# One folded weight by seven half-block products per pair of rows, in an mLSTM cell followed by a multiplicative feed-forward kernel

## The chip, the core and the metric

The kernel runs on one core of a Trainium2 chip. The metric is the device time of one execution in microseconds (us). Engines are named as the profile names them: PE is TensorE's matrix multiply and PEld its weight loads, DVE is VectorE, ACT is ScalarE, POOL is GpSimd, SP is the engine that issues most DMAs. PSUM is the memory that PE writes its results to.

## The reference, cut to what matters

The first half is a recurrent cell over 768 time steps for 4 batches of 8 heads of width 40. The second half is a feed-forward block with weights alone between its products:

```
C = f_stab * C + i_stab * outer(v_t, k_t);  n = f_stab * n + i_stab * k_t
y_t = sigmoid(o_t) * (C q_t) / max(|n . q_t|, 1)
...
x = y as (3072 tokens, 320)
a = x @ w1            # w1, w2: 320 x 1024
b = x @ w2
h = a * b @ w3        # (a * b) @ w3, w3: 1024 x 1024
return h @ w_out      # w_out: 1024 x 320
```

There is nothing between `w3` and `w_out`, so the kernel computes the product `w3 @ w_out` once (1024 x 320, "the folded weight", `w3o`) and applies it to `a * b`.

## The kernel before, in words

**Tiling.** The cell is computed chunkwise: 24 units of 128 time steps of one batch (6 chunks of time by 4 batches). The feed-forward block has 6 groups of 512 tokens. `up` and `up_rest` compute a and b for two 128-row slices of the 1024 and 256 tokens: two products of 128 rows per slice in `up`, and the last 64 of the 320 rows in `up_rest`, which packs four 64x64 products into the array at once. The result `ab` is multiplied into the output by `w3o` in `ffn_out`. Groups 3 to 5 are computed in another way (`up_by_seven`, `out_by_seven`): a 2x2 split of the matrices, whose product is made of seven half-size products and 15 sums instead of eight products (Strassen's method in Winograd's form). Every PE product in float32 shows in the trace as two weight loads and two matmul records; a transpose shows as one of each.

**Folding.** `w_out` lies in `wo`, eight tiles of 128 rows. `w3` arrives in 16 half tiles of 64 rows (the weights are 64-bit floats in memory: `fetch` issues the DMAs, four for a half of `w3`, into one of four `raw` buffers; `scale` works on both words on ACT; `to_f32` joins them on DVE, L199 and L200). `convert` then turns a half of `w3` on DVE (L248) into `w3T[ko]`; there are two `w3T` buffers. One step after both halves of a tile are turned, `fold` makes its 128 rows of the folded weight: eight products 128x128 by 128x320 that accumulate in one PSUM tile (`w3_mm`), and one ACT copy into `w3o` (L264). Eight tiles give 64 products, 128 records.

**Stages and order.** A loop over 32 steps s overlaps everything. In step s, PE does in order: transposes of y of an earlier unit (`x_trans`, px), the folds, output products, the `up` blocks, their `up_rest`, and then `quarter_work`, which has the cell's many small products for units s and s-1. The lists below give how many blocks, output products and conversions each step has:

```python
n_up = [0] * 2 + [1] * 4 + [2] * 10 + [0] * 16
n_down = [0] * 16 + [2] * 5 + [1] * 4 + [0] * 7
n_cvt = [0, 0, 2, 0, 1, 2, 3, 3, 3] + [2] * 6
```

PE runs in the order in which the program is written (`in_order` adds an ordering dependency between each two products), and `keep_order` does the same for the other engines at the end. `issue_after` only places instructions behind a given one in that order; it adds no wait across engines. So each engine is a queue that runs in program order, and a wait at its head holds what stands behind it. The conversions of step s come at its end, and DVE does them while PE is in step s+1. A step's weights are fetched four conversions ahead (`fetched < converted + 4`).

**PSUM.** Before step 24 the `mps` tiles (pa, pb, px, wp, po) share four banks; a tile takes the bank that is free the longest and waits until its last reader is done with it. The reader of pa is ACT (a_sb, L638), of pb it is DVE (ab, L639).

**POOL** has, in each step of this part: a state update (L335) that waits for DVE's update of the state, the weighted v for the next unit (vw, L330), a small copy of y (L476), two causal masks on pw for the next unit (L308), and the state update at the head of the next step.

In the profile of before, `quarter_work`'s products begin on PE at 48.2 us in step 4, 55.8 in step 5, 93.1 in step 8, 105.4 in step 9, 125.8 in step 10, 141.1 in step 11, 203.0 in step 15 and 218.2 in step 16.

Of the kernel before, what the change touches and what calls it, by code (L numbers as in the profile page):

```python
# [8 lines left out]
FP = mybir.dt.float32  # L9
# [7 lines left out]
def kernel(  # L17
# [59 lines left out]
    def mps(shape, name):  # L77
        pool = banks.pop(0)
        banks.append(pool)
        return pool.tile(shape, FP, name=name, tag="m")  # L80
# [10 lines left out]
    def mm(out, lhsT, rhs, start=True, stop=True):  # L91
        in_order(nc.tensor.matmul(out, lhsT=lhsT, rhs=rhs, start=start, stop=stop))  # L92
# [135 lines left out]


    w3T_t = {}  # L230
    turned_w3, ready_w3 = [], []

    def scale_next(early=False):
        scaled.append(pend.pop(0))
# [2 lines left out]
    def convert():  # L237
        if not scaled:
            scale_next()
        dst, raw, ko, half = scaled.pop(0)  # L240
        if dst is not None:
            to_f32(dst, raw)
            return
        w3 = wst.tile([128, CW], FP, name="w3", tag="w3")
        to_f32(w3, raw)
        if half == 0:
            w3T_t[ko] = wst.tile([128, FO, 128], FP, name="w3T", tag="w3T")
        nc.vector.transpose(out=w3T_t[ko].rearrange("c k (m r) -> c m k r", r=32)[:, 2 * half:2 * half + 2],  # L248
                            in_=w3.rearrange("r (m c k) -> r m k c", m=2, k=FO))
        if half:  # L250
            turned_w3.append(ko)

    def fold():
        while ready_w3:
            w3_mm(ready_w3.pop(0))
        ready_w3.extend(turned_w3)
        turned_w3.clear()

    def w3_mm(ko):
        w3T = w3T_t.pop(ko)  # L260
        wp = mps([128, DM], "wp")
        for ki in range(FO):
            mm(wp, w3T[:, ki, :], wo[:, ki, :], start=(ki == 0), stop=(ki == FO - 1))
        nc.scalar.mul(out=w3o[:, ko, :], in_=wp, mul=UP ** -2)  # L264


    qT_t, kT_t, vw_t, before_t, y_t, x_t = {}, {}, {}, {}, {}, {}
# [65 lines left out]
    def decayed(new, old, n, x):  # L333
        c, b = divmod(n, B)
        nc.gpsimd.tensor_tensor(out=new, in0=old, op=OP.mult, in1=decay[:, b * NP:(b + 1) * NP, 2 * c + x:2 * c + x + 1]  # L335
                                .to_broadcast([P, NP, D1]))
# [281 lines left out]
    def up(gr, fs, cs):  # L618


        if gr not in ab_t:
            ab_t[gr] = [ffn.tile([128, FO, 2 * P], FP, name="ab", tag="ab", bufs=6) for _ in range(2)]
        x, n = x_t[gr], cs.stop - cs.start
        pa, pb = mps([128, len(fs), n], "pa"), mps([128, len(fs), n], "pb")
        for p, wt in ((pa, w1), (pb, w2)):
            for i, f in enumerate(fs):
                for cc in range(KF):
                    mm(p[:, i, :], wt[:, cc, f * 128:(f + 1) * 128], x[:, cc, cs], start=(i == cc == 0), stop=False)
        return pa, pb, x, gr, fs, cs

    def up_rest(pa, pb, x, gr, fs, cs):
        for i, f in enumerate(fs):
            for j, e in quarters:
                mm((pa, pb)[j][halves[e], i, :], wr[halves[j], f * 128 + e * L:f * 128 + (e + 1) * L],
                   x[halves[j], KF, cs], start=False, stop=(i == len(fs) - 1))
        j, t0 = divmod(cs.start, 2 * P)
        a_sb = ffn.tile([128, len(fs), cs.stop - cs.start], FP, name="a_sb", tag="a_sb")
        nc.scalar.mul(out=a_sb, in_=pa, mul=UP ** -2)  # L638
        nc.vector.tensor_tensor(out=ab_t[gr][j][:, fs[0]:fs[-1] + 1, t0:t0 + a_sb.shape[-1]], in0=pb, in1=a_sb, op=OP.mult)  # L639
# [90 lines left out]

        return single, shared, left, product

    def ffn_out(blocks, pos=None):

        pos = pos or [mps([P, DM], "po") for _ in blocks]
        for (gr, j), po in zip(blocks, pos):
            for f in range(FO):
                mm(po, ab_t[gr][j // 2][:, f, j % 2 * P:(j % 2 + 1) * P], w3o[:, f, :], start=(f == 0), stop=(f == FO - 1))
        for (gr, j), po in zip(blocks, pos):
            o_sb = ffn.tile([P, DM], FP, name="o_sb", tag="o_sb", bufs=2)  # L740
            nc.scalar.copy(out=o_sb, in_=po)  # L741
            t0 = j * S + gr * P
            nc.scalar.dma_start(out=out[t0:t0 + P, :], in_=o_sb)


    KH, NH = FO // 2, DM // 2

    def out_weight_sums():

        T_o.extend(m[:, i * KH * NH:(i + 1) * KH * NH].rearrange("p (f n) -> p f n", n=NH)  # L750
                   for m, i in ((v_all, 0), (gates, 0), (gates, 1), (q_all, 0)))
        (B11, B12), (B21, B22) = ([w3o[:, k * KH:(k + 1) * KH, i * NH:(i + 1) * NH] for i in range(2)] for k in range(2))
        T1, T2, T3, T4 = T_o
        for dst, p, q in ((T1, B12, B11), (T2, B22, T1), (T3, B22, B12), (T4, B21, T2)):
            yield nc.gpsimd.tensor_tensor(out=dst, in0=p, in1=q, op=OP.subtract)

    T_o, S_o = [], {}
    wsums = out_weight_sums()

    def quarters_of_ab(gr, j):  # L760
        return [[ab_t[gr][j][:, k * KH:(k + 1) * KH, t * P:(t + 1) * P] for k in range(2)] for t in range(2)]
# [49 lines left out]
    n_out = [0] * 27 + [1, 0, 1, 0, 3]  # L811
    w12 = [("w12", i, part) for part in range(2) for i in range(2 * KF + 1)]
    todo = w12[5:] + [("wo", i, 0) for i in range(FO)] + [("w3", ko, part) for ko in range(FO) for part in range(2)]
    n_cvt = [0, 0, 2, 0, 1, 2, 3, 3, 3] + [2] * 6
    n_fetch = [5, 5, 10]
    pinned, ahead = 32, 9
    behind = ExitStack()
# [2 lines left out]
    for s in range(len(n_up)):  # L820
# [21 lines left out]
        if s < NU:  # L842
            if s >= B:
                decayed(state[s % B][1], state[s % B][0], s, 0)
        if s == 2 or N_DVE < s < NY + 2:
            twice(s - 2)
        if NY <= s - 2 < NU:
            get_back(s - 2)
        while s >= N_DVE and turned < min(s - 2, NY):
            x_trans(turned)  # L850
            turned += 1
        fold()
        if s >= len(n_up) - 2:
            ab_sums(*summed.pop(0))
        def pairs():
# [13 lines left out]
            seven[1]()  # L869
        if seven and s <= NU:  # L870
            ffn_out([downs.pop(0) for _ in range(n_down[s])], [cell[1][:, i, 0:DM] for i in range(2)])
        else:
            for _ in range(n_down[s]):
                ffn_out([downs.pop(0)])
# [2 lines left out]
        if seven and s > NU:  # L877
            seven[0]()
        now = [ups.pop(0) for _ in range(n_up[s])]
        open_ups = [up(*x) for x in now] if s != 2 else []  # L880
        if s == 3:
            turn(3)
        def rest():
            for x in open_ups:
                up_rest(*x)
            if seven:
                seven[2]()
            if s == 3:
                scale_next()
                scale_next()  # L890

        def between():
            twice(1)
            weighted(2)
            rows_of_u(3)
            for _ in range(3):
                scale_next()
            for n in range(2):
                x_trans(n)
                if n == 0:  # L900
                    warm(1, small=38)
            for _ in range(3):
                convert()
            turn(2)
            block = up(*now[0])
            weighted(3)
            weights(3)
            masks(3)
            out_gate(2)
            convert()  # L910
            up_rest(*block)

        gated = None
        if s <= NU:
            gated = quarter_work(s, rest, between if s == 2 else None, convert if s == 3 else None)
        else:
            rest()
        with tc.issue_after(gated.ins) if gated else nullcontext():
            if seven:
                seven[3]()  # L920
            for _ in range({NU: 1, NU + 1: 3}.get(s, 0)):
                next(wsums)
            if s == NU + 1:
                ab_sums(*summed.pop(0))
            if NY <= s - 2 < NU:
                x_turn(s - 2)
            for n in () if s == 1 else (s + 2,) if s < B else (s + 2, s + 3) if s == B else (s + 3,):
                if n < N_U:
                    rows_of_u(n)
            if N_DVE <= s + 1 < NU:  # L930
                gated = turn(s + 1)
            if s - 2 in range(4 * GT - 1, NU, GT):
                token_sums((s - 2) // GT)
            if s < len(n_up) - 2 and n_out[s + 1] and s > NU + 2:
                ab_sums(*summed.pop(0))
# [28 lines left out]
        if s == B:  # L964
            for i, r in enumerate(third):
                nc.sync.dma_start(out=U_d[i * GC:(i + 1) * GC].rearrange("c r t -> r c t"), in_=U3[r])
        with tc.issue_after(gated.ins) if N_DVE <= s + 1 < NU else nullcontext():
            for _ in range(n_cvt[s] if s < len(n_cvt) else 0):
                convert()
                converted += 1  # L970
# [9 lines left out]
            for ins in keep_order(front):  # L980
                behind.enter_context(tc.issue_after(ins))
    behind.close()
    assert not ups and not sevens and not downs and not outs and not summed and not todo and not pend and not turned_w3 and not ready_w3, (len(ups), len(downs), len(todo), len(pend))
# [1 line left out]
_INS = ['q', 'k', 'v', 'i_gate', 'f_gate', 'o_gate', 'moe_w1', 'moe_w2', 'moe_w3', 'moe_w_out']  # L985
_OUTS = [((3072, 320), 'float32')]
# [25 lines left out]
```

## Time and profile before

| what | value |
|---|---|
| time, median of 3 runs | 426.7 us (424.85, 426.7, 532.37) |
| profiled execution, its own time | 427.89 us |
| its span, first to last instruction | 425.8 us |
| granted TensorE clock over the span | 0.996 |
| PE busy | 414.1 us, 97% of the span, 5353 records |
| DVE / POOL / ACT busy | 74% / 36% / 35% |
| the fold, wp<-wo,w3T | 128 records, 35.9 us busy |
| up_rest, pa and pb<-xT,wr | 768 records, 73.4 us busy |
| w3o<-wp on ACT (L264) | 8 copies, 438 ns each |
| w3T<-w on DVE (L248) | 16 turns, 1111 ns each |
| instruction DMAs (queue q8) | 42 packets, 0.69 MB |
| mean DMA rate | 120 GB/s; 183 GB/s from 30 to 108 us |

In an answer of the trace, a row of the timeline has the start in us, the length in us, the engine, the line, the operation, out<-in, the shape and the number of records that were merged. A bracket at its end gives how long the engine was idle just before, and what ended that. Matmul records overlap, so a row is longer than the time that it adds: the distance between the starts of two rows is the time PE gave to the first. "issue" is time in which an engine waited for nothing that the profile shows. Line numbers are those of the kernel before.

### The profile page before, as it was taken

How to read it: one execution, taken by the hardware profiler on the slowest of the kernel's cores; microseconds unless marked ns; L12 is line 12 of the kernel's file. 1: busy time of each engine (PE TensorE's matmuls, PEld its weight loads, DVE VectorE, ACT ScalarE, POOL GpSimd, SP SyncE). 2: the span in 40 equal slices, each digit the busy share in tenths (PEclk: the TensorE clock that was granted, in tenths of full speed). 3: DMA queues.
4: the chain of work that ended last, by engine and by line, in shares of the span. 5: the costliest groups of instructions: out<-in, count | busy, mean ns of one | idle time of the engine just before them, and what ended most of it. 6: DMA issues, size and time to landing. Idle time of an engine off the chain costs nothing.

```text
span 425.8 us, 13079 instructions
## 1 busy us (share of the span) xinstructions
PE 414.1 (97%) x5353; PEld 335.3 (79%) x5353; DVE 313.5 (74%) x635; ACT 150.1 (35%) x404; POOL 154.3 (36%) x211
## 2 busy tenths in 40 slices
PE   7989989999999999999999999999999999999996
PEld 4768878888688788787777778788778879888896
DVE  6676986888949779778736966596868699575971
ACT  4766865567723623630433313032311110210000
POOL 4421342233303303303307751546453587542100
PEclk9989999999999999999999999999999999999999
DMA  8999998598977776985425675756421120000001
GB/s 186 204 173 245 214 144 140 134 193 180 215 183 154 166 182 135 181 164 105 89 80 130 153 141 121 142 133 117 87 44 36 35 39 2 31 2 31 2 32 62
DMA packets 135211, 51.15 MB, mean 120 GB/s; under 512 B 109360, under 2 KB 126960, under 8 KB 135152
## 3 DMA queue, kind: packets, MB, share of 16 engines
q1 hardware_dynamic: 131552, 46.29, 53.9%
q10 hardware_dynamic: 3600, 4.03, 2.7%
q8 instruction: 42, 0.69, 0.7%
q14 instruction: 17, 0.14, 0.1%
HBM read 44.50 MB, written 5.80 MB: 118 GB/s over the span
## 4 chain that ended last, share of the span: by engine, by line
PE 53%; issue 20%; DVE 7%; POOL 7%; SPq 7%; DMA 5%; ACT 1%; POOLq 0%; DVEq 0%
PE cell L92 17%; PE pa L92 12%; PE o L92 8%; PE pb L92 8%; PE p L92 3%; POOL pw L308 3%; SPq L184 3%; DVE w3T L666 2%; PE pt L95 1%; POOL vw L330 1%; SPq L148 1%; DMA raw<-in_moe_w_dram 1%; PE fill L92 1%; POOL raw L659 1%; POOL state L335 1%
## 5 line engine op out<-in xcount | busy, mean ns | idle before, releaser
L335 POOL TENSOR_TENSOR state<-state,decay 128x164 f32<-128x164 f32 x40 | 20.0, 500 | 154.8 <-DVE state L404 129.0
L92 PE MATMUL pa<-xT,w 128*128 128x256 f32 x240 | 60.4, 382 | 0.0
L92 PEld LDWEIGHTS pa<-xT,w 128*128 128x128 f32 x240 | 44.4, 190 | 6.8 <-DVE h L430 0.4
L303 ACT ACTIVATE pw<-pw,aT 128x64 f32<-128x64 f32 x184 | 46.4, 339 | 3.2 <-ACT o_sb L741 1.9
L92 PE MATMUL pb<-xT,w 128*128 128x256 f32 x192 | 45.4, 379 | 0.0
L729 POOL TENSOR_TENSOR ab<-ab,a_sb 128x512 f32<-128x512 f32 x22 | 29.4, 1356 | 32.2 <-DVE ab L684 32.2
L92 PEld LDWEIGHTS pb<-xT,w 128*128 128x128 f32 x192 | 36.4, 190 | 5.0
L711 POOL TENSOR_TENSOR wo<-wo 128x512 f32<-128x512 f32 x22 | 27.4, 1268 | 29.8 <-DVE wo L686 29.8
L92 PE MATMUL pa<-xT,wr 64*64 64x256 f32 x384 | 37.0, 386 | 0.5 <-DVE wr L200 0.5
L92 PE MATMUL wp<-wo,w3T 128*128 128x320 f32 x128 | 35.9, 433 | 1.1 <-DVE ab L639 0.6
L308 POOL TENSOR_SCALAR_AFFINE_SELECT pw<-pw 64x512 f32<-64x512 f32 x48 | 35.8, 746 | 3.0 <-ACT pw L303 1.2
L92 PE MATMUL pb<-xT,wr 64*64 64x256 f32 x384 | 36.4, 380 | 0.0
L92 PE MATMUL cell<-w3o,ab 128*128 128x320 f32 x128 | 35.4, 432 | 0.0
L638 ACT ACTIVATE a_sb<-pa 128x512 f32<-128x512 f32 x24 | 14.3, 598 | 59.0 <-PE pb L92 59.0
L639 DVE TENSOR_TENSOR ab<-pb,a_sb 128x512 f32<-128x512 f32 x24 | 16.4, 688 | 23.2 <-ACT a_sb L638 22.8
L92 PEld LDWEIGHTS wp<-wo,w3T 128*128 128x128 f32 x128 | 23.8, 190 | 10.5 <-DVE ab L639 0.8
L92 PEld LDWEIGHTS cell<-w3o,ab 128*128 128x128 f32 x128 | 24.3, 190 | 9.5
L92 PEld LDWEIGHTS pa<-xT,wr 64*64 64x64 f32 x384 | 18.9, 132 | 15.4 <-issue 8.8
L686 DVE SCALAR_TENSOR_TENSOR a_sb<-pa,wo 128x512 f32<-128x512 f32 x12 | 8.3, 689 | 29.8 <-PE pa L92 29.8
L430 DVE TENSOR_TENSOR h<-cell,h 64x164 f32<-64x164 f32 x88 | 28.6, 326 | 1.6
L92 PE MATMUL po<-w3o,ab 128*128 128x320 f32 x96 | 26.4, 433 | 0.0
L92 PEld LDWEIGHTS po<-w3o,ab 128*128 128x128 f32 x96 | 18.1, 190 | 7.3
(180 smaller groups left out, 846.4 us busy)
## 6 DMA issues: line engine op xcount, KB each, us to landing
raw<-in_moe_w_dram SPq DMA_DIRECT2D x64, 128.0 KB, 3.4
kbuf<-in_k_dram SPq DMA_DIRECT2D x24, 160.0 KB, 4.5
v_all<-in_v_dram SPq DMA_DIRECT2D x24, 160.0 KB, 4.9
o_in<-in_o_gate_dram SPq DMA_DIRECT2D x24, 160.0 KB, 4.8
pw<-U_d SPq DMA_DIRECT2D x28, 128.0 KB, 3.5
raw<-in_moe_w_dram SPq DMA_DIRECT2D x5, 512.0 KB, 6.7
raw<-in_moe_w_out_dram SPq DMA_DIRECT2D x8, 320.0 KB, 4.1
gates<-in_k_dram SPq DMA_DIRECT2D x28, 80.0 KB, 2.5
```

Of the source, the lines that this page charges most:

```text
L92: in_order(nc.tensor.matmul(out, lhsT=lhsT, rhs=rhs, start=start, stop=stop))
L184: nc.sync.dma_start(out=dst, in_=src)
L303: nc.scalar.activation(out=pw[:, h, :], in_=src[:, h, :], func=AF.Exp, bias=aT[:, c, b * H + h:b * H + h + 1])
L308: nc.gpsimd.affine_select(out=pw[r], in_=pw[r], compare_op=OP.is_ge, fill=0.0, base=0, pattern=[[0, H], [1, L]], channel_multiplier=-1)
L335: nc.gpsimd.tensor_tensor(out=new, in0=old, op=OP.mult, in1=decay[:, b * NP:(b + 1) * NP, 2 * c + x:2 * c + x + 1] .to_broadcast([P, NP, D1]))
L430: nc.vector.tensor_tensor(out=part, in0=ph[x][halves[e]], in1=part, op=OP.add)
L638: nc.scalar.mul(out=a_sb, in_=pa, mul=UP ** -2)
L639: nc.vector.tensor_tensor(out=ab_t[gr][j][:, fs[0]:fs[-1] + 1, t0:t0 + a_sb.shape[-1]], in0=pb, in1=a_sb, op=OP.mult)
L666: nc.vector.tensor_tensor(out=dst, in0=p, in1=q, op=OP.subtract)
L686: nc.vector.scalar_tensor_tensor(out=out, in0=p, scalar=UP ** -2, in1=q, op0=OP.mult, op1=OP.add)
L711: aside_by.tensor_tensor(out=kept[j][:, 1:4:2], in0=kept[j][:, 1:3], in1=kept[j][:, 3:4].to_broadcast([128, 2, TH]), op=OP.add)
L729: aside_by.tensor_tensor(out=t[:, f:FO:FH, :], in0=t[:, f:FO:FH, :], in1=a, op=OP.mult)
```

## The change

**The fold.** The rows of `w3o` are made in four pairs i of tiles (2i, 2i+1) by the seven-product method. The 2x2 split is: two tiles, two halves of the 1024 (four products deep each), and two halves of the 320 columns. Each of the seven products is four PE products 128x128 by 128x160. The parts are:

- four sums of `wo` on POOL, once (`fold_weight_sums`, each 128x640: two in step 8, two in step 9). One of them overwrites a quarter of `wo`, one lies in the memory of `w3o`'s last pair until that pair is made; for that pair the fourth sum is made again (`fold_last_sum`, step 15).
- four sums of `w3T` on POOL per pair (`fold_sums`, each 128x512, steps 9, 11, 13, 15). One overwrites a part of `w3T`; the others lie in the `ab` memory of group 2 before that is used, and for the last pair in two `raw` buffers.
- `fold_first(i)`: two of the seven products, behind `quarter_work` of steps 9, 11, 13 and 14, and one ACT copy.
- `fold_second(i)`: the other five, 20 PE products, behind the first `up` block and its `up_rest` of steps 10, 12, 14, and behind the first part of the output products of step 16; two ACT copies; and five sums, on POOL for the first three pairs and on DVE for the last.

**Moved with it.** In steps 10, 12 and 14 the first block's `up_rest` follows its `up` at once instead of standing behind the second block's `up`. `x_trans` of units 7, 9 and 11 moves from the head of a step to behind `quarter_work` of the step before. In step 16 the output products over the last two of eight tiles follow `quarter_work`. The `w3` buffer before the turn is one instead of two, and the output's staging tile lies in the memory of the sums of `wo`.

**One conversion** moves from step 8 to step 5, and with it the fetches of steps 5 to 8, which follow the number of conversions.

**The last rows** of the first blocks (steps 2, 3 and 4) are computed in two parts of 128 columns instead of one of 256.

```diff
-    def fold():
-        while ready_w3:
-            w3_mm(ready_w3.pop(0))
...
-    def w3_mm(ko):
-        w3T = w3T_t.pop(ko)
-        wp = mps([128, DM], "wp")
-        for ki in range(FO):
-            mm(wp, w3T[:, ki, :], wo[:, ki, :], start=(ki == 0), stop=(ki == FO - 1))
-        nc.scalar.mul(out=w3o[:, ko, :], in_=wp, mul=UP ** -2)
+    def fold_weight_sums():
...
+        for dst, p, q in ((T1, B12, B11), (T2, B22, T1), (T4, B21, T2), (B12, B22, B12)):
+            yield nc.gpsimd.tensor_tensor(out=dst, in0=p, in1=q, op=OP.subtract)
+
+    def fold_sums(i):
...
+        (A11, A12), (A21, A22) = rows_of_w3(i)
...
+        for dst, p, q, op in ((S1, A21, A22, OP.add), (S2, S1, A11, OP.subtract), (A21, A11, A21, OP.subtract),
+                              (S4, A12, S2, OP.subtract)):
+            nc.gpsimd.tensor_tensor(out=dst, in0=p, in1=q, op=op)
+
+    def fold_first(i):
+        A11, A12 = (w3T_t[2 * i][:, k * KH:(k + 1) * KH] for k in range(2))
+        (B11, _), (B21, _) = halves_of(wo)
+        wp = fold_products(((A11, B11), (A12, B21)))
+        return lambda: nc.scalar.mul(out=fold_of(i)[:, 0:3:2], in_=wp, mul=UP ** -2)
+
+    def fold_second(i):
...
+        wp, wq = mps([128, 3, NH], "wp"), mps([128, 2, NH], "wq")
+        for p, x, a, b, first, last in ((wq, 1, A22, T4, True, False), (wp, 0, S1, T1, True, False), (wp, 1, S2, T2, False, False),
+                                        (wp, 2, S3, T3, False, True), (wq, 0, S4, B22, False, True)):
+            for k in range(KH):
+                mm(p[:, x], a[:, k, :], b[:, k, :], start=(first and k == 0), stop=(last and k == KH - 1))
...
+        nc.scalar.mul(out=M1, in_=wp, mul=UP ** -2)
+        nc.scalar.mul(out=M2, in_=wq, mul=UP ** -2)
+
+        def adds(by=nc.gpsimd):
+            for out, p, q in ((C[:, 1], M1[:, 1], C[:, 0]), (C[:, 0], C[:, 0], C[:, 2]), (C[:, 2], M1[:, 2], C[:, 1]),
+                              (C[:, 1:4:2], C[:, 1:3], M1[:, 0:1].to_broadcast([128, 2, NH])), (C[:, 1:3], M2, C[:, 1:3])):
+                by.tensor_tensor(out=out, in0=p, in1=q, op=OP.add)
...
-    def up_rest(pa, pb, x, gr, fs, cs):
+    def up_rest(pa, pb, x, gr, fs, cs, parts=1):
+        n = (cs.stop - cs.start) // parts
         for i, f in enumerate(fs):
-            for j, e in quarters:
...
+            for t in range(parts):
+                for j, e in quarters:
+                    mm((pa, pb)[j][halves[e], i, t * n:(t + 1) * n], wr[halves[j], f * 128 + e * L:f * 128 + (e + 1) * L],
...
-    n_cvt = [0, 0, 2, 0, 1, 2, 3, 3, 3] + [2] * 6
+    n_cvt = [0, 0, 2, 0, 1, 3, 3, 3, 2] + [2] * 6
...
+        elif s == 16:
+            finish = ffn_out([downs.pop(0) for _ in range(n_down[s])], split=FO - 2)
+            fold_second(FO // 2 - 1)(nc.vector)
...
+        if s in (10, 12, 14):
+            up_rest(*up(*now.pop(0)))
+            adds.append(fold_second((s - 10) // 2))
...
+                up_rest(*x, parts=2 if s in (3, 4) else 1)
...
+        if s == 16:
+            finish()
+        if s in (9, 11, 13):
+            x_trans(turned)
+            turned += 1
+        if s in (9, 11, 13, 14):
+            first_copy = fold_first((s - 8) // 2)
         with tc.issue_after(gated.ins) if gated else nullcontext():
...
+            if s in (8, 9):
+                next(fsums), next(fsums)
+            for x in adds:
+                x()
+            if s in (9, 11, 13, 15):
+                fold_sums((s - 9) // 2)
```

## The prediction

> **What bounds the kernel now.** I read the engine totals first, then PE's waits, then PE's timeline step by step. Totals, and the stretch in which the fold lies (start:end us, length, busy per engine with records, clock, DMA share, GB/s):
>
> ```profile
> PE 414.1 (97%) x5353; PEld 335.3 (79%) x5353; DVE 313.5 (74%) x635; ACT 150.1 (35%) x404; POOL 154.3 (36%) x211
> ...
> 108.00:205.00 97.00, 96.12 (x1281) 77.14 (x1282) 74.47 (x142) 39.14 (x102) 20.69 (x36) 1.00 0.76 159
> ```
>
> PE idles 0.9 us of these 97, at full clock; POOL has 76 us free. So time here is the sum of PE's records, and an edit pays if it takes records from PE without making it wait. One step without a stall:
>
> ```profile
> 127.66 0.55 PE L95 MATMUL px<-ident,y 128*128 128x128 f32 x3
> 128.04 4.47 PE L92 MATMUL wp<-wo,w3T 128*128 128x320 f32 x16
> 132.35 1.89 PE L92 MATMUL pa<-xT,w 128*128 128x256 f32 x8
> 134.08 1.89 PE L92 MATMUL pb<-xT,w 128*128 128x256 f32 x8
> ```
>
> By starts, px gives PE 0.38 us of work, a tile's fold 4.31 (16 records, 269 ns each), a block's up 3.46. The breaks in PE's stream that this change touches:
>
> ```profile
> 107.65 1.24 DVE L639 TENSOR_TENSOR ab<-pb,a_sb 128x512 f32<-128x512 f32 x2
> ...
> 108.35 1.07 PE L92 MATMUL wp<-wo,w3T 128*128 128x320 f32 x3 [0.58 <-DVE ab L639]
> ...
> 59.05 0.23 PEld L92 LDWEIGHTS cell<-vw,kbuf 64*40 64x40 f32 x12 [1.60 <-issue]
> ...
> 96.51 0.27 PE L95 MATMUL pt<-ident,q_all 128*128 128x128 f32 x1 [0.30 <-issue]
> ...
> 144.57 3.93 PE L92 MATMUL wp<-wo,w3T 128*128 128x320 f32 x14 [0.54 <-issue]
> ```
>
> The first is a PSUM bank: wp waits for DVE's ab, which stands behind step 8's third conversion (its turn of w3T ends at 107.72). From px at 107.22 to wp at 108.35 is 1.13, 0.75 more than usual. The others wait for no engine: they start at 57.37, 95.94 and 143.61, and exceed normal spacing by 1.7, 0.5 and 0.75. In the recorded stream of PE (loads and products) they stand before records 1985, 3265 and 4545, which are 193 + 256 x 7, x 12, x 17. Queue q8 brings 42 packets, 0.69 MB, so 16 KB each. These are instruction refills.
>
> [...] 160-column records follow each other faster than a 190 ns load.
>
> ```profile
> 381.37 2.34 PE L92 MATMUL o<-gates,kbuf 128*128 128x160 f32 x16
> 383.55 1.25 PE L92 MATMUL o<-w3o,ab 128*128 128x160 f32 x8
> ```
>
> That is 2.18/16 = 136 ns. [...]
>
> ```profile
> 364.67 0.59 PE L92 MATMUL pa<-w3T,w 128*128 128x256 f32 x2
> 365.10 0.59 PE L92 MATMUL pb<-xT,raw 128*128 128x256 f32 x2
> 365.63 1.09 PE L92 MATMUL pa<-xT,wr 64*64 64x256 f32 x16
> ...
> 367.51 0.70 PE L92 MATMUL p<-xT,w 128*128 128x256 f32 x2
> 368.05 0.38 PE L92 MATMUL p<-w3T,raw 128*128 128x256 f32 x1
> ```
>
> A pair takes 0.43; before wr it takes 0.53, after it 0.54, and the 32 wr records take 1.88 against 1.71 to 1.73 in their own mode: together 0.36 for a round trip. [...] vw takes 0.73 mostly, but 1.18 at 46.69. [...]
>
> **The change part by part.**
>
> *Fold products.* Removed: 128 records x 269 = 34.5. Added: 4 pairs x 28 products x 2 = 224 records x 136 = 30.5. PE gains 4.0.
>
> *Mode changes.* In steps 10, 12 and 14 the first block's wr stands between products of the full array. Three round trips x 0.36 = +1.1. Elsewhere the new parts join changes that exist.
>
> *x_trans moved* from the heads of steps 10, 12, 14: the same records. The copy on ACT now runs under fold_first (16 x 136 = 2.2 us), which covers its 0.47; without that up would wait some 0.6. Nothing.
>
> *Conversion moved.* In step 5 DVE's third conversion of wo (0.52 + 0.62) and ACT's two passes (2 x 0.49) meet an idle DVE: 2.93 before ab at 69.43. Nothing; without that idle, 1.1. In step 7 two of three are now w3 (2.3 against 1.15), so ab is 1.1 late; its bank is asked for 2 us later, covered. In step 8 DVE loses 2.3 us, so the 0.75 at 107.5 goes: -0.75. The next reader there is fold_first itself, for the same ab, which is then 1 us early. Its fetch, four DMAs, moves from step 8 to before step 7's loads: past pw, kbuf, q_all, v_all and o_in on SP (1.8 us of issue, about 2.6 us of transfer, 0.5 MB at 200 GB/s). SP stood idle from 71.05 to 77.99, and kbuf, issued at 84.17 and landing in a median 5.0, is read by PE at 95.29: 6 us spare. Nothing. On POOL no DMA is moved.
>
> *Sums on POOL.* Per pair 4 x 1.27 (row L711, 128x512), once 4 of 128x640 at 1.5 to 2.0 (four rows of L755), adds of 3 x 0.47 + 2 x 0.73. All 24+ us fit into POOL's free time; what counts is when. Behind the sums on POOL stand vw and the masks of the next unit, read 6 us or more later. Behind px, POOL's state update ends 3.2 us later (94.90 to 98.08 in step 8). In step 9 two weight sums (4.0) and four sums (5.1) follow: S1 at 8.5, S4 at 12.3, some 0.4 later [...]. PE: px 0.38, fold_first 2.2, up 3.55, wr 1.0, so fold_second starts at 7.2, its first product needs T4 alone; it would take S1 at 8.3 and S4 at 11.6. S4 is 0.7 to 1.1 late: +1.0 (bounds 0 and 3.7, the latter with POOL at vw's 1.6 times). For steps 12 and 14 the weight sums are absent, S4 comes at 8.7, and nothing is late.
>
> *Waits on DVE.* Its turn of w3T in step 9 overwrites what the sums read, so waits for S4: about 4 us. Behind it stand a conversion and the first block's ab. In the built order the second block's pb takes the bank that ACT frees, not this ab's; ab is needed by px of step 11, 3 us later. Nothing; in other cover up to 1.4.
>
> *ACT* gets 4 more copies and wider ones, 2.3 us over seven steps at 35% busy. Nothing.
>
> *Step 16.* PE leaves the last two tiles open until DVE's five adds: M1 copied 0.7 after its product (1.1 before fold_second ends), then 3 x 0.33 + 2 x 0.49 and gaps: done about as quarter_work (1.9) ends. +0.2, bounds 0 and 1.
>
> *Last rows in two parts.* 24 products become 48 of half the length. [...] 64-column products already keep pace with their loads. +0.1, bounds 0 and 0.3.
>
> *Refills.* The trace's refill starts 2 to 3.4 us after PE is 64 records ahead of a block, 6.5 at worst (56.6), takes 1.1, and is used 1.4 later: about 5 us, 8.8 at worst. So a block of short records breaks the stream. The work of the three broken ones (64 records and the block) is 7.1, 4.1 and 4.1 us; the next whole one had 5.0. Parts and fold shift the numbering by 96 and 192: in the built program the short ones are in steps 5 (7.2), 6 (5.4), 9 (4.75), 13 (4.5) and 14 (4.85). The one in step 5 meets the same loaded DMA: 1.4; the rest 0.4 + 0.7 + 0.6 + 0.2. Sum 3.3 against 3.0: +0.3, bounds -3.0 and +5.
>
> Sum: -4.0 + 1.1 - 0.75 + 1.0 + 0.2 + 0.1 + 0.3 = -2.0. The profiled execution took 427.9 (span 425.8 and 2.1 around it) and becomes 425.9; the median of 426.7, lower by 1.2, becomes **424.7**.
>
> **Rivals.** (1) The gain is eaten at the fold: [...] S4 is 3.7 late in step 10, not 1.0: 424.7 + 2.7 = 427.4. For it: vw at 1.18; against: 22 sums on L711 averaged 1268. (2) Slower, by refills: five short blocks stand in the loaded half. If a refill takes 6.5 us, the five breaks are 0, 1.1, 1.75, 2.0 and 1.65; with step 5's at its worst 1.6 they make 8.1, 4.8 over my 3.3: 429.5. It decides above 5.5 us; against it are the typical 5 us after 90 us. (3) The numbering falls well and no refill or sum is late: -4.0 + 1.1 - 0.75 + 0.3 - 3.0 = -6.3: 420.4. That the products are not shortened is excluded by the 136 ns.
>
> **Chances.** Forecast 424.7 (422.5 to 426.3): 0.60; gain eaten, about 427.4: 0.19; refills, 428 to 432: 0.15; better, to 420.4: 0.06. The range 421.5 to 429.5 leaves out half of the last two and little else. 2% is 8.5 us, about what a measurement of this kernel can tell from no change: faster needs below 418.2, slower above 435.2. No case reaches the first; the second takes refills near the worst and a stall together, 0.06.
>
> **What would show it.** wp and wq with 224 records at 136 ns; no wp wait for ab near 107; rows "issue" on PE near 57 and 105 to 175, and their sum; PE waiting for POOL's sums in step 10 alone; PE busy about 2.5 us less. I am wrong if 160-column records run slower, if POOL's sums hold PE in steps 12 or 14, or if DVE, held by S4, holds PSUM banks.

## The result, and the profile after

The changed kernel takes 430.26 us, median of 20 runs, against 426.8 us for the kernel before: a ratio of 1.0076, 95% interval 1.0051 to 1.0102, so 2.2 to 4.4 us more. One run of each kernel, at 532.37 and 603.92 us, fell in a slow state and is left out of the ratio. The prediction had 424.7, with a range to 429.5. The profiled execution of the changed kernel took 433.0 us (span 431.3), 2.7 above its median. Where those 2.7 lie is seen below: in the start-up.

Engine totals of the changed kernel: busy time, share of the span, number of records.

```profile
PE 417.5 (97%) x5497; PEld 347.2 (81%) x5497; DVE 328.6 (76%) x640; ACT 152.1 (35%) x408; POOL 199.4 (46%) x247
```

The same stretch as in the prediction, 108 to 205 us, in the view of stretches (start:end us, length, busy per engine with records, in the order PE, PEld, DVE, ACT, POOL, then clock, DMA share, GB/s):

```profile
108.00:205.00 97.00, 92.70 (x1329) 80.97 (x1322) 83.39 (x140) 41.14 (x106) 55.09 (x65) 0.98 0.71 158
```

PE was to be 2.5 us less busy, and shows 3.4 more. It idles 4.3 us of these 97, where it idled 0.9. DVE has 8.9 more to do in them (83.39 against 74.47) and POOL 34.

These two moments are not at the same work, so I cut both executions at three starts that mean the same in both: the second px, the last px ahead of the fold, and the first of the 32 output products that follow the fold. Before, the start-up and the stretch of the fold:

```profile
0.00:28.41 28.41, 23.92 (x407) 15.98 (x407) 20.61 (x53) 17.02 (x51) 11.98 (x41) 0.94 0.94 182
...
94.90:231.03 136.13, 134.72 (x1835) 106.73 (x1827) 99.50 (x194) 56.58 (x152) 35.89 (x57) 1.00 0.70 150
```

The same two after:

```profile
0.00:31.65 31.65, 28.01 (x408) 19.69 (x408) 20.79 (x53) 17.04 (x51) 12.73 (x42) 0.84 0.94 186
...
98.06:236.44 138.38, 134.09 (x1932) 114.20 (x1924) 113.37 (x198) 57.92 (x154) 80.62 (x93) 0.99 0.68 146
```

The start-up took 31.65 against 28.41: 3.2 us of the 5.5 between the spans. In it PE ran at a clock of 0.84, against 0.94 before. In the profiled executions of the experiments, most of which have the start-up of one of the two kernels unchanged, the same px comes at 25.7 to 29.6. So this belongs to the one execution and not to the change. What the change costs stands in the stretch of the fold, 138.38 against 136.13. DVE is 13.9 us busier in it.

PE's timeline of the changed kernel, fold products only (start, length, engine, line, operation, tile and operands, count, and in brackets the idle time ahead with what ended it):

```profile
112.29 4.12 PE L92 MATMUL wp<-wo,w3T 128*128 128x160 f32 x16 [1.83 <-DVE ab L707]
...
145.74 2.44 PE L92 MATMUL wp<-wo,w3T 128*128 128x160 f32 x16 [1.16 <-DVE ab L707]
...
153.78 2.34 PE L92 MATMUL wp<-fold_m,ab 128*128 128x160 f32 x16
155.96 1.25 PE L92 MATMUL wp<-wo,w3T 128*128 128x160 f32 x8
...
177.10 2.44 PE L92 MATMUL wp<-wo,w3T 128*128 128x160 f32 x16 [1.16 <-DVE ab L707]
```

Two lines in the middle show that the products take what was forecast: 155.96 - 153.78 = 2.18 for 16 records, 136 ns each. The other three are fold_first of steps 9, 11 and 13. Each waits for ab, with which DVE reads a block's pb; that it waits for the PSUM bank of pb is tested in experiment 1. By starts, from px to wp, the three take 2.37, 1.71 and 1.70 where 0.38 is normal: 2.0, 1.3 and 1.3 lost. Of these, only a wait of 0.75 had stood in the kernel before, and that one was to go.

The first is also longer than the other two, 4.12 against 2.44. PE's clock between 112 and 116 (third number from the right):

```profile
112.00:116.00 4.00, 3.71 (x16) 3.71 (x17) 3.73 (x12) 1.25 (x5) 0.19 (x1) 0.60 0.76 207
```

The breaks that I take for refills of PE's instructions cost less than forecast in this execution. That they are refills is an inference from counts: queue q8, which the profile lists as "instruction", brings 42 packets in the execution before and 43 in this one, and PE has 10706 and 10994 records of loads and products in them, 41.8 and 42.9 times 256. The breaks of 1.7 near 57, of 0.5 near 96 and of 0.7 near 143 are gone, and there is one new one, at the end of step 6, where one packet of q8 starts between 71 and 73; on PE's load side:

```profile
74.11 0.19 PEld L92 LDWEIGHTS cell<-vw,kbuf 64*40 64x40 f32 x9 [1.54 <-issue]
```

The account of the profiled executions, after less before, in us. "Read" is from starts of PE's groups of records:

| term of the prediction | predicted | read |
|---|---|---|
| fold products, mode changes, step 16 (-4.0 + 1.1 + 0.2) | -2.7 | -2.5 |
| wait of wp for ab | -0.75 | +3.9 (2.0 + 1.3 + 1.3 - 0.75) |
| POOL's sums late in step 10 | +1.0 | +0.3, and 1.7 of half clock ahead of it |
| refills | +0.3 | -1.25 (1.64 new; 1.74, 0.46 and 0.69 gone) |
| last rows in two parts | +0.1 (an estimate) | +0.03 (925 ns against 914, three times) |
| start-up | 0 | +3.2, this execution |
| behind the fold | 0 | +0.1 |
| sum | -2.0 | +5.5 |

The first "read" is what remains of the stretch's +2.25 when 6.6 of waits and half clock in it after, and 1.9 of waits before, are taken off; so the column must add up, and that it does proves nothing. Without the start-up the sum is +2.3, at the low end of the measured 2.2 to 4.4. So the question for the experiments is why ab is late, three times.

**Step 9.** DVE in the changed kernel, from the unit's o_in to ab:

```profile
102.56 1.58 DVE L508 SCALAR_TENSOR_TENSOR o_in<-o_in,den 128x320 f32<-128x320 f32 x1
104.17 1.72 DVE L510 TENSOR_TENSOR y<-h,o_in 128x320 f32<-128x320 f32 x1
...
106.91 1.10 DVE L200 CUSTOM_DVE_ANT_0 w<-raw,w 128x1024 uint16<-128x1024 uint16 x1
...
111.59 1.25 DVE L707 TENSOR_TENSOR ab<-pb,a_sb 128x512 f32<-128x512 f32 x2
```

The same two operations in the kernel before:

```profile
98.35 0.76 DVE L443 SCALAR_TENSOR_TENSOR o_in<-o_in,den 128x320 f32<-128x320 f32 x1
99.15 0.49 DVE L445 TENSOR_TENSOR y<-h,o_in 128x320 f32<-128x320 f32 x1
```

And POOL beside them in the changed kernel:

```profile
102.23 1.56 POOL L266 TENSOR_TENSOR fold_m<-wo 128x640 f32<-128x640 f32 x1
103.87 1.67 POOL L266 TENSOR_TENSOR fold_m<-wo,fold_m 128x640 f32<-128x640 f32 x1
```

o_in and y take 2.05 longer, and each ends 0.35 after one of POOL's two subtractions. Not all of DVE's work is stretched: the transposition kT takes 1.13 beside a sum of POOL (at 119.83; POOL from 119.52, 1.56) where it took 1.10 before. What sets the two kinds apart is not shown. From o_in to ab DVE needs 9.0 us with two conversions; before it needed 9.3 with three, and one conversion is 2.3.

**Steps 11 and 13.** DVE in the changed kernel, from the ab of step 10 to that of step 11:

```profile
132.09 0.69 DVE L707 TENSOR_TENSOR ab<-pb,a_sb 128x512 f32<-128x512 f32 x1 [2.04 <-ACT a_sb L706]
132.69 0.49 DVE L488 TENSOR_TENSOR h<-cell,gT 128x328 f32<-128x328 f32 x1
...
145.04 1.25 DVE L707 TENSOR_TENSOR ab<-pb,a_sb 128x512 f32<-128x512 f32 x2
```

The same work in the kernel before, with the last row of its conversions:

```profile
127.31 0.49 DVE L423 TENSOR_TENSOR h<-cell,gT 128x328 f32<-128x328 f32 x1
...
137.90 1.11 DVE L248 STREAM_TRANSPOSE w3T<-w 128x512 f32<-128x512 f32 x1
141.13 0.69 DVE L639 TENSOR_TENSOR ab<-pb,a_sb 128x512 f32<-128x512 f32 x1 [2.12 <-ACT a_sb L638]
```

Before, a step of PE had 15.3 us (px at 127.66 and 142.95) and DVE's work in it left 2.1 idle ahead of ab. Now the whole fold of a pair, apart from fold_first, stands in the even steps; from px at 133.05 to px at 144.03 there are 11.0 us. DVE's work from h to ab, two conversions in it, is 12.35 (132.69 to 145.04), with one gap of 0.5 in it, for POOL's state update. The same work, with the same gap, took 11.7 before (127.31 to 139.01). So of the 1.3 that PE loses here, some 0.7 is the shorter step alone and 0.65 a DVE that is slower beside POOL: the five adds of fold_second now stand ahead in POOL's queue, so vw and a state update fall on the conversions, whose second steps take 1.11 and 0.84 where they took 0.69 each. No run takes these two halves apart.

### The profile page after: what moved, and what is told of

Read it like the earlier page. It is cut to its first block, busy times and chain, and to the rows that moved or that the text cites. A ratio compares the mean times of both kernels' runs of the same rounds, so it can differ in the third digit from the quotient of the medians.

```text
span 431.3 us, 13427 instructions
## 1 busy us (share of the span) xinstructions
PE 417.5 (97%) x5497; PEld 347.2 (81%) x5497; DVE 328.6 (76%) x640; ACT 152.1 (35%) x408; POOL 199.4 (46%) x247
## 4 chain that ended last, share of the span: by engine, by line
PE 82%; DVE 7%; issue 3%; DMA 3%; SPq 2%; POOL 2%; ACT 0%; DVEq 0%; POOLq 0%
PE cell L92 21%; PE pa L92 20%; PE pb L92 13%; PE o L92 8%; PE p L92 4%; PE wp L92 4%; PE po L92 3%; PE fill L92 2%; PE wq L92 2%; PE pt L95 2%; DVE w3T L734 2%; PE px L95 1%; DVE pw L851 1%; POOL ab L284 1%; DMA kbuf<-in_k_dram 1%
## 5 line engine op out<-in xcount | busy, mean ns | idle before, releaser
L92 PE MATMUL pa<-xT,wr 64*64 64x256 f32 (+1 forms) x408 | 37.7, 374 | 0.5 <-DVE wr L200 0.5
L92 PE MATMUL pb<-xT,wr 64*64 64x256 f32 (+1 forms) x408 | 37.1, 368 | 0.0
L92 PEld LDWEIGHTS pb<-xT,wr 64*64 64x64 f32 x408 | 20.9, 133 | 3.0
L510 DVE TENSOR_TENSOR y<-h,o_in 128x320 f32<-128x320 f32 x24 | 20.7, 861 | 0.8
```

The source lines that it names most:

```text
L510: yield nc.vector.tensor_tensor(out=y_t[n][:, 0:DM].rearrange("p (h d) -> p h d", d=D), in0=h[:, :, 0:D], in1=e, op=OP.mult)
```

## The experiments

All ratios are to the kernel before, measured beside it. The medians of before in the two rounds of runs were 426.0 and 425.8, against 426.8 beside the changed kernel; so an experiment is compared with the changed kernel by the two ratios (1.0076 for the changed kernel, with an interval of 1.1 us either way).

**1. fold_first ahead of px.** Is it the bank, and what comes next when the wait goes?

```diff
-        if s in (9, 11, 13):
-            x_trans(turned)
-            turned += 1
         if s in (9, 11, 13, 14):
             first_copy = fold_first((s - 8) // 2)
+        if s in (9, 11, 13):
+            x_trans(turned)
+            turned += 1
```

> The changed kernel with the order of two items turned round at the ends of steps 9, 11 and 13: fold_first stands ahead of x_trans, so that wp takes the bank that ACT's a_sb frees and px the one that DVE's ab frees. Bank theory (wp waits because its bank is the one that DVE's ab still reads: 2.05, 1.39 and 1.39 us in these three steps): the three waits ahead of wp go, since the 2.2 us of wp now lie over the rest of DVE's work. Steps 11 and 13 gain 2.8. In step 9 the gain of 2.0 comes back as a wait for POOL's fourth sum in step 10 (0.3 before, then about 2.3), since POOL follows DVE and not PE. So 430.3 - 2.8 = 427.5, ratio to the kernel before about 1.002. Rival, that PE is held by DVE as such and not by a bank: the wait only moves on to px, 430.3. Rival on record, refills of instructions: no wait for ab is worth anything, 430.3.

Measured: 428.85 us, ratio 1.0071 (1.0040 to 1.0102). In its PE timeline no wp waits for ab; these rows come in its place, in steps 9 and 10:

```profile
108.49 1.99 PE L92 MATMUL pa<-xT,w 128*128 128x256 f32 x8 [0.57 <-ACT xT L551]
...
116.20 2.71 PE L92 MATMUL wp<-fold_m,ab 128*128 128x160 f32 x16 [1.69 <-POOL ab L284]
```

The bank theory holds for wp: with DVE as late as ever, wp starts right behind the unit's last group of records (104.55, and wp at 104.97). The time does not show the 2.8 us expected: by the ratios it is 0.2 less than in the changed kernel, which is within the intervals. The trace says why. px is now the last thing ahead of pa, and pa waits 0.57 for ACT's copy of xT (0.7 by starts), in each of the three steps; the prediction had named this price. In step 10 the gain of step 9 is more than given back: PE loses 3.1 to POOL's sums, which start behind a state update that DVE makes late.

**2. One conversion moved out of each short step.**

```diff
-    n_cvt = [0, 0, 2, 0, 1, 3, 3, 3, 2] + [2] * 6
+    n_cvt = [0, 0, 2, 0, 1, 3, 3, 3, 2, 3, 1, 3, 1, 2, 2]
```

> The changed kernel with one conversion of w3 moved from PE's step 11 to step 10 and one from step 13 to step 12 (n_cvt 3, 1, 3, 1 in place of 2, 2, 2, 2 for steps 9 to 12). Theory that in the steps without fold_second PE is 4.3 us shorter than DVE's unchanged work: DVE loses 2.3 us in steps 11 and 13, so the two waits of 1.39 ahead of wp go; the one of 2.05 in step 9 stays. 430.3 - 2.8 = 427.5, ratio to before about 1.002. If DVE's lateness comes from elsewhere (POOL's sums), or if refills are what costs: 430.3.

Measured: 426.52 us, ratio 1.0016 (0.9996 to 1.0037): by the ratios 2.6 us less than the changed kernel, where 2.8 was expected. PE in steps 9 to 11:

```profile
110.71 2.44 PE L92 MATMUL wp<-wo,w3T 128*128 128x160 f32 x16 [1.85 <-DVE ab L707]
...
119.54 2.71 PE L92 MATMUL wp<-fold_m,ab 128*128 128x160 f32 x16 [0.63 <-POOL ab L284]
...
142.83 2.34 PE L92 MATMUL wp<-wo,w3T 128*128 128x160 f32 x16
```

In step 11 wp follows px at once (142.45), and in step 13 too. That settles that DVE's work is what was late there; as a conversion is 2.3 us, it does not tell which of the two halves of the 1.3 made it late. The wait of step 9 stays, as it should. The clock stayed whole behind it in this execution, and PE then stood for POOL's sums instead: by starts wq, wp and wp take 0.9, 0.6 and 0.6 more than their work, 2.1 together. So half clock and this wait are two forms of one loss: POOL is 2 us late for step 10, and a slow PE does not notice.

**3. Without the first two weight sums.**

```diff
-        fold_T.extend((T1, T2, B12, T4))
-        for dst, p, q in ((T1, B12, B11), (T2, B22, T1), (T4, B21, T2), (B12, B22, B12)):
+        fold_T.extend((B11, B22, B12, T4))
+        for dst, p, q in ((T4, B21, B22), (B12, B22, B12)):
...
-            if s in (8, 9):
+            if s in (9,):
```

> The changed kernel without the two weight sums T1 and T2, which POOL makes beside DVE's step 8 unit; the quarters B11 and B22 of wo stand in their place in the products, so this part of the fold is not computed. [...] (POOL's long subtractions slow VectorE's instructions beside them): DVE's o_in and y go back from 1.58 and 1.72 to 0.76 and 0.49, the first conversion behind them by another 0.4; ab comes 2.5 us sooner, at about 11.0 after px of step 8 in place of 13.5; the wait of 2.06 ahead of wp in step 9 goes, and the half clock that follows it, if it is a consequence. 430.3 - 2.05 = 428.2, or 426.4 with the clock. Rival (DVE is late in step 9 through its two conversions of w3 alone): the wait stays at 2.0, 430.3.

The kernel leaves these two sums out, so a part of the folded weight is not computed. Measured: 426.84 us, ratio 1.0027 (1.0008 to 1.0045), by the ratios 2.1 less than the changed kernel. DVE, and then PE in steps 9 and 10:

```profile
99.23 0.49 DVE L510 TENSOR_TENSOR y<-h,o_in 128x320 f32<-128x320 f32 x1
...
106.16 2.34 PE L92 MATMUL wp<-wo,w3T 128*128 128x160 f32 x16
...
114.43 2.71 PE L92 MATMUL wp<-wo,ab 128*128 128x160 f32 x16 [0.17 <-POOL ab L284]
...
118.91 1.35 PE L92 MATMUL wq<-wo,ab 128*128 128x160 f32 x8 [0.36 <-POOL ab L284]
```

y is back at 0.49, o_in at 0.76. From o_in to ab DVE needs 6.45 (98.43 to 104.88) in place of 9.03, so two subtractions of 1.6 on POOL had cost DVE 2.6. wp follows px (105.78) without a wait, and the clock stays whole. In step 10 PE now loses 1.6 by starts to POOL's sums, though DVE is not late: so a part of the gain is spent there. The waits of steps 11 and 13 are still there, 1.3 each.

**4. The two subtractions alone, in the kernel before.**

```diff
+            if s == 8:
+                for part in range(2):
+                    nc.gpsimd.tensor_tensor(out=w3o[:, 6:8].rearrange("p k n -> p (k n)").rearrange("p (f n) -> p f n", n=NH),
+                                            in0=wo[:, 4 * part:4 * part + 4, NH:DM], in1=wo[:, 4 * part:4 * part + 4, 0:NH], op=OP.subtract)
             if NY <= s - 2 < NU:
                 x_turn(s - 2)
```

> The kernel before with nothing but two subtractions of 128x640 added to POOL in step 8, at the place where the changed kernel makes T1 and T2; they read wo and write a part of w3o that is written again later. [...] beside them DVE's o_in and y (0.76 and 0.49) take about 1.6 and 1.7, its conversions 0.4 more; ab, at 107.65, comes 2.5 later, and the wait of PE ahead of wp grows from 0.58 to about 3.1, with the clock at half for some microseconds after it: 426.8 + 2.5 = 429.3, or 431 with the clock. Rival: POOL's work alone costs nothing, 426.8, and DVE's rows keep their times.

Measured: 428.70 us, ratio 1.0079 (1.0050 to 1.0108), 2.7 us more for 3.2 us of work on an engine that is busy for 36% of the span. DVE and PE in the timeline:

```profile
97.75 1.73 DVE L445 TENSOR_TENSOR y<-h,o_in 128x320 f32<-128x320 f32 x1
...
107.96 5.46 PE L92 MATMUL wp<-wo,w3T 128*128 128x320 f32 x13 [2.87 <-DVE ab L639]
```

The stretch behind the wait:

```profile
108.00:112.00 4.00, 4.00 (x9) 2.66 (x10) 3.42 (x12) 2.46 (x4) 0.53 (x2) 0.57 0.85 217
```

From o_in to ab DVE takes 11.1 where it took 9.3. By starts PE loses 3.0 between px and wp, not 0.75; of these 2.3 more, 0.5 come from PE itself, which in this execution has no break of 0.5 near 96 and so is there sooner. Then the clock falls to 0.57, and the 32 records of wp take 10.4 where they took 8.7. Nothing waits for the result of the two subtractions, and no row of PE waits for POOL: what they cost comes through DVE, and in this execution through the half clock behind its wait.

**5. Conversions spread, and the four weight sums behind the masks.** The losses of steps 9 and 10 come from POOL's sums and from a late DVE; can the sums stand where they cost less?

```diff
-    n_cvt = [0, 0, 2, 0, 1, 3, 3, 3, 2] + [2] * 6
+    n_cvt = [0, 0, 2, 0, 1, 3, 3, 3, 2, 3, 1, 3, 1, 2, 2]
...
-            if s in (8, 9):
-                next(fsums), next(fsums)
...
                 masks(s + 1)
             if s != 2:
                 out_gate(s)
+            if s == 8:
+                for _ in range(4):
+                    next(fsums)
```

> The changed kernel with the conversions spread as in the second experiment (3, 1, 3, 1 in steps 9 to 12), and all four weight sums on POOL in one go at the end of step 8, behind that step's masks, instead of two behind each state update of steps 8 and 9. If it is the place of POOL's sums that costs: DVE's o_in and y of that step keep 0.76 and 0.49, only its conversions run beside POOL, so ab is some 1.5 sooner and the wait ahead of wp in step 9 falls from 2.0 to about 0.6; and S1 to S4 begin right behind the state update of step 9, 3.3 sooner than now, so that PE no longer waits for them in step 10 (2.2 in the second experiment). 426.5 - 1.4 - 2.2 = 422.9, ratio to before 0.993. Rival, that DVE loses as much wherever POOL's sums stand, and that the sums then hold POOL's state update: 426.5 or more.

Measured: 424.45 us, ratio 0.9967 (0.9944 to 0.9990): faster than both kernels, by 1.4 us against the one before. DVE, and PE in step 9:

```profile
107.47 1.82 DVE L200 CUSTOM_DVE_ANT_0 w<-raw,w 128x1024 uint16<-128x1024 uint16 x1
...
110.36 1.26 DVE L707 TENSOR_TENSOR ab<-pb,a_sb 128x512 f32<-128x512 f32 x2
...
111.08 2.44 PE L92 MATMUL wp<-wo,w3T 128*128 128x160 f32 x16 [1.14 <-DVE ab L707]
```

PE's wait ahead of wp is 1.3 by starts, from 2.0, and no product waits for POOL in step 10. Half of the rival is true: o_in and y keep their times, but the conversions now bear it, 1.82 in place of 0.69 in this line. ab itself runs beside a subtraction of POOL (110.66 to 112.20) and takes 1.26 for its two, against 1.25 in the changed kernel. Of the 1.55 us over the expected 422.9 this may explain 0.7 (a wait of 1.3 where 0.6 was expected); the rest is within the interval and is not settled.

**6. The conversion moved alone, in the kernel before.**

```diff
-    n_cvt = [0, 0, 2, 0, 1, 2, 3, 3, 3] + [2] * 6
+    n_cvt = [0, 0, 2, 0, 1, 3, 3, 3, 2] + [2] * 6
```

> The kernel before with the one conversion moved alone (n_cvt 3, 3, 3, 2 in place of 2, 3, 3, 3 for steps 5 to 8). By the prediction DVE has 2.3 us less ahead of ab at 107.65, so the wait of PE ahead of wp (0.75 over its normal spacing) goes and nothing else moves: 426.0 - 0.75 = 425.3, ratio 0.998, with no wait for ab in step 10. Rival, that the conversion is missed elsewhere (three of them in PE's step 6 hold that step's ab by 1.1, or its fetch delays a load): 426.0 to 427.1, with a new wait between 60 and 84.

Measured: 426.87 us, ratio 0.9998 (0.9978 to 1.0018). The wait for ab is gone, and DVE idles 4.0 ahead of it. The interval holds the 425.3 expected and most of the rival's range. And this is not the clean part that I took it for: the first tile of w3 is turned a step sooner, so the loop also folds it a step sooner, and step 10 then has one tile and this row:

```profile
113.17 1.99 PE L92 MATMUL pa<-xT,w 128*128 128x256 f32 x8 [1.28 <-ACT xT L486]
```

The copy of xT stands on ACT behind eight passes of the conversions (108.21 to 112.77). In this execution the gain of 0.75 is spent there. Whether the move would gain anything without that is not shown.

**7. The last rows in one part again.**

```diff
-                up_rest(*x, parts=2 if s in (3, 4) else 1)
+                up_rest(*x, parts=1)
...
-            up_rest(*block, parts=2)
+            up_rest(*block)
```

> The changed kernel with the last rows of the first up blocks in one part, as before; 48 products and 48 loads fewer. On PE the three parts cost 10 ns each (925 against 914 ns), so nothing by themselves. Refill theory (a break stands where a short block of 256 instructions begins, at the 193rd of each 256 records of loads and products): the numbering is then that of the kernel before up to the fold, so the break of 1.6 at the end of step 6 goes and those of 1.7 near 57 and 0.5 near 96 come back, records 1985 and 3265: 430.3 + 0.6 = 430.9. Rival, that breaks have nothing to do with the numbering: the one near 72 stays and 430.3 does too.

Measured: 429.02 us, ratio 1.0074 (1.0041 to 1.0107), which does not tell it from the changed kernel. Its breaks do:

```profile
58.55 0.23 PEld L92 LDWEIGHTS cell<-vw,kbuf 64*40 64x40 f32 x12 [2.15 <-issue]
...
98.40 0.27 PE L95 MATMUL pt<-ident,q_all 128*128 128x128 f32 x1 [1.00 <-issue]
```

The one near 72 is gone and these two are back, before records 1985 and 3265 of PE's stream (counted with its semaphore instructions), as foretold; two more, of 0.9 at 142.8 and 1.5 at 164.1, stand before records 4545 and 5057. All four are 193 + 256k. So 96 records of a kind that costs 0.03 us move the places where the stream breaks. The size of a break is another matter. Experiment 4 has the PE stream of before, with a break of 0.3 near 57 and none near 96; experiments 2 and 5 have that of the changed kernel, with a break of 0.7 and 1.2 before record 1729 (193 + 256 x 6) that the changed kernel's own profile lacks. In time the shift comes to nothing here: the later two breaks fall at the ends of steps 11 and 12, and the waits for ab in steps 9, 11 and 13 shrink to 0.9, 0.4 and 0.

**8. The conversion put back in the changed kernel.**

```diff
-    n_cvt = [0, 0, 2, 0, 1, 3, 3, 3, 2] + [2] * 6
+    n_cvt = [0, 0, 2, 0, 1, 2, 3, 3, 3] + [2] * 6
```

> The changed kernel with the conversion put back (n_cvt 2, 3, 3, 3 for steps 5 to 8). By the theory that DVE is what PE waits for in step 9: one conversion more ahead of ab there, 2.3 us, so the wait ahead of wp grows from 2.05 to 4.3, POOL's sums of step 10 come 2.3 later too, and the time is 430.3 + 2.3 = 432.6, ratio to before about 1.015. Rival, that the wait comes from POOL alone or from refills: 430.3.

Measured: 432.15 us, ratio 1.0143 (1.0091 to 1.0195), four runs; by the ratios 2.9 more than the changed kernel, where 2.3 was expected. PE in step 9:

```profile
112.33 4.11 PE L92 MATMUL wp<-wo,w3T 128*128 128x160 f32 x16 [3.26 <-DVE ab L707]
```

From px to wp PE loses 3.4 us, in place of 2.0, with half clock behind it (a mean of 0.65 from 113 to 117); 4.3 was expected. Steps 11 and 13 keep their 1.3. So the move that stands in the change is worth having in it, some 2 to 3 us, though it does not remove the wait.

## Why the prediction was wrong

**What failed: the wait of wp for ab.** The step reads "so the 0.75 at 107.5 goes: -0.75. The next reader there is fold_first itself, for the same ab, which is then 1 us early", and for the wp of steps 11 and 13 the sum has no term at all (*x_trans moved* ends in "Nothing"). Read are +3.9 in the place of -0.75. Two things were left out.

- The two sums that POOL makes in step 8 were charged to POOL alone. I took the slowing of two engines beside each other as a price on POOL's rows alone (vw at 1.18) and never asked what DVE pays. It pays 2.6 us for 3.2 of POOL's (experiment 3; 1.8 in the kernel before, experiment 4). That turns an ab that is "1 us early" into one that is 1.7 after px.
- fold_first was moved to the ends of steps 9, 11 and 13, and fold_second into the steps between. I moved the records and did not recompute the length of each step for DVE. A step of 15.3 became one of 11.0, with 12.35 of DVE's work in it. Where DVE idled 2.1 ahead of ab in step 11 of before, the bank is now 1.3 late; with one conversion less in the step that wait is gone (experiment 2). About half of the 1.3 is the first omission again, a DVE slower beside POOL; that share is read from the trace alone.

**What was mis-sized.** *Sums on POOL*: +1.0, bounds 0 and 3.7. It is 1.6 where DVE is not late and the clock is whole (experiment 3), with S4 done 13.1 after px where 12.3 and "some 0.4 later", an estimate, were given; and 2.1 where the state update ahead of them also comes from a late DVE (experiment 2). In steps 12 and 14 nothing is late, as said. DVE's wait for S4 was 1.2 where 4 was given, and held no bank. *Refills*: +0.3, and -1.25 was read. The places were right (experiment 7); of the short blocks named, only that of step 6 broke the stream, by 1.6 where it was given 0.4, and the one of step 5, given 1.4, did not. But -1.25 compares one execution with one: over the six profiles with the changed numbering (the changed kernel, experiments 1, 2, 3, 5 and 8) the breaks add up to 1.3 to 2.9, and in before and experiment 4 to 2.9 and 0.9. So no saving in refills is shown, and a bound of what a refill takes is too crude to be added up to a tenth.

**What held.** 224 records at 136 ns, and the mode changes: in experiment 2 the two steps from px at 142.45 to px at 172.38 have no wait and take 29.93, where two clean steps of before take 2 x 15.29; 0.65 less for a pair, and the prediction's terms give 1.0 - 0.36. Nothing was lost at step 16, and the two parts cost 0.03. Together -2.5, as a remainder, for -2.7. The price of 0.6 that px would pay without fold_first behind it was measured as 0.57 (experiment 1).

**The rivals.** "Slower, by refills" gave 429.5, near the 430.3, and is not the cause: it needed breaks of 8.1 in sum, and none of the six profiles has more than 2.9. That its number came near is luck. "The gain is eaten at the fold" named the place, but the engine in it was POOL, late with its sums; it was DVE first, slowed by POOL. The half clock was in no case.

**What stays open.** Of the measured +3.5 the trace explains 2.3; the rest is within the interval, and no part of the change is shown to carry it. Breaks for refills that differ by 2 us from one execution of a PE stream to another (2.9 in before, 0.9 in experiment 4) are enough for it, but were read in one execution of each kernel only.

## What to carry to other kernels

Work that is put on an idle engine is not free if another engine is slower beside it: two POOL subtractions of 1.6 us each cost DVE 2.6 us here (experiment 3), so price them by what DVE loses, too. When products are moved between steps, write down each step's new length against the unchanged work of every other engine in it, and ask for each PSUM bank which engine frees it and when. Here two conversions moved from short steps to long ones were worth as much (2.6 us) as the shorter products and their mode changes (2.5).

## What the runs showed of the hardware that I had not expected

- Behind some stops of PE its granted clock was half for about 3.4 us: in the changed kernel behind a stop of 2.0 (0.50 from 112.83 to 116.23; a mean of 0.60 from 112 to 116), where 16 records of wp take 4.12 against 2.44, 1.7 more; in experiment 4 behind 3.0 (0.57 from 108 to 112); in experiment 5 behind a break of 1.7 (0.53 from 72.6 to 76); in experiment 8 behind a break of 2.2 (0.72 from 70 to 76) and a wait of 3.4 (0.65 from 113 to 117). The means of these experiments come to 3.2 to 3.4 us each, if the clock was half as in the changed kernel. Stops of 2.0 in experiment 2 (1.00 from 108 to 120), of 1.7 in before (1.00 from 50 to 108) and of 1.7 in experiment 3 (a mean of 0.999 over its span) were not followed by it. That the stop is its cause is not shown: no run changes the one and holds the other.
- Beside POOL's subtractions DVE's y went from 0.49 to 1.72, o_in from 0.76 to 1.58 (changed kernel, and experiment 4 within 0.01), a conversion's first step from 0.43 to 1.20 and its second from 0.69 to 1.82 (experiment 5); in experiment 5 a transposition (1.13) and ab (two in 1.26) did not change.
